# Gated linear attention and a token/channel mixer on one core: batch 0 by token slot, its u made transposed, another token order, other weight pieces, a new order of the work

## The chip, the cores and the metric

The kernel runs on one core of a Trainium2 chip. The core has TensorE (PE in the profile; its weight loads are PEld), VectorE (DVE), ScalarE (ACT), GpSimd (POOL) and SyncE (SP), each with its own in-order queue, and DMA engines that move data between HBM and SBUF. TensorE writes to PSUM, which the kernel splits into eight banks of 512 fp32 values per partition. The metric is the device time of one launch in microseconds (us); a kernel's time is the median of its runs.

## The reference

Four batches, eight heads, 768 tokens, head size 48. First a recurrence with a decay per key channel, then a mixer over tokens and channels, both with a residual:

```python
state = zeros((B, H, D, D))
for t in range(S):
    state = alpha[:, :, t, :, None] * state + einsum('bhd,bhe->bhde', k[:, :, t], v[:, :, t])
    y[:, :, t] = einsum('bhd,bhde->bhe', q[:, :, t], state)
x = y.transpose(0, 2, 1, 3).reshape(B, S, H * D)              # 4 x 768 x 384
h = relu(x.T @ w_tok1) @ w_tok2                               # 768 -> 256 -> 768, per batch
u = x + h.T
out = u + relu(u @ w_ch1) @ w_ch2                             # 384 -> 1536 -> 384
```

Inputs and output are fp32; the kernel computes its products in bf16 with fp32 sums.

## The kernel before

**Attention.** The tokens of a batch are cut into three chunks of 256 (`n` = 0 to 11 over four batches; batch 0 has chunks 0, 1 and 2). Partition p of a chunk holds tokens 2p and 2p+1, its two *slots*; partitions 0 to 63 are the first half of 128 tokens, 64 to 127 the second. Per chunk: load alpha, k, q, v (`ld_at`, `ld_kt`, `ld_qt`, `ld_vt`, 384 KB each); logarithms of alpha on ACT (`ln`); running sums of them by a triangular matmul (`cum`, in batch 0 `cumw` for both slots at once); exponentials `E` and `IE`; keys and queries scaled by them (`kk`, `qq`, line 700); transposes of both (`trk`, `trq` on PE in chunks 0 to 5; `dk`, `dq` by DMA later) and copies into `tpk` and `tpq` (`evk`, `evq`, later `pq`); scores `G` per half of 128 tokens, multiplied with a mask on DVE into `gtm` (`mask`, line 770); `y` = masked scores times v, plus the earlier state's part (`ia`, `ib`); `x` is the copy of y in bf16. `K` sums keys times values per half. The state is either `s` (times the decay, line 837), or an add (`sa`, line 841) followed by a product (`sm`, line 844) where there is an earlier state.

So that K and y can contract over all 128 partitions of one half of the tokens, values and keys of a half must lie on 128 partitions: `vs` (two copies of 64 partitions of v) and `ka`, `kb`, `kc` (of the scaled keys) move them, on ACT, POOL or DVE.

**Mixer.** Per batch: `t1` (12 matmuls, x with w_tok1) and `ht` (relu); `t2` (12, ht with w_tok2); `u` (add of x, on DVE); the transpose of u into `ut`; `c1` (24 groups of three matmuls of 384 columns, each a channel block `mc` of 12 and a half of the tokens) and `rt` (relu, on ACT or DVE, line 873 or 875); `c2` (six token blocks in four groups of three) and `o` (add of u, line 911); `st` (store). In batch 0 the transpose of u runs on PE (`up`, line 894) with three copies; in the others it is a DMA transpose (`ux`, line 729).

**Weights** are loaded as fp32 in 16 pieces of 384 KB into the buffers of the inputs and cast to bf16 (`ldw`, `cw`). w_ch1 comes in six pieces of 128 rows by 768 columns, so a channel block of c1 waits for three pieces.

**Order.** All instructions stand in one written list (`ORDER`), where each name ends in its engine: t is PE, s ACT, v DVE, g POOL, y SP. An engine takes its own names in this order and waits at each for its inputs; so a name that waits holds back all of its engine's names behind it. `BUFS` gives the buffer of every value in the order of first use: an instruction that writes into a buffer also waits for the last user of what was there (a PSUM bank, an input buffer). `shared` (line 732) makes POOL's SBUF work and the DVE's that is marked with `port` take turns in list order. All loads and DMA transposes, and some stores, are issued from SP's queue, the other stores from ACT's. `f1` to `f12` are dummy matmuls on zeros (the fill; up to four of 384 columns in fp32 and the rest of 512 in bf16), each before the matmul that it names; `fN` has N // 3 in fp32, each of which the profile records as two, and N % 3 in bf16.

## Time and profile before

| | |
|---|---|
| median of 3 runs | 163.48 us (163.34 to 164.39) |
| span of the profiled execution, first to last instruction | 160.5 us |
| the profiled execution's own time beside its span | not given; the median lies 3.0 us above the span |
| PE busy | 154.6 us, 96% |
| DVE, ACT, POOL busy | 114.9, 97.8, 80.8 us |
| HBM read, written | 25.17 MB, 4.72 MB |
| granted TensorE clock | 1.00 |

A row of the profile names the line, the engine, the operation, what it writes and reads (`out<-in`, buffer numbers left out) with partitions x elements and types, how many there were, then busy time, mean duration in ns, the idle time of the engine before them and what ended it. In rows in order of time the first two numbers are the start in the span and the length in us, and the bracket holds the idle time before. Matmuls are pipelined, and their recorded lengths overlap: their rate is read from their starts. Line 643 is a helper that issues most matmuls of the attention, so these are told apart by their tiles.

### The profile page before, as it was taken

Reading aid. Unit: us, or ns where it says so; the run is one execution under the profiler, and the core shown is the slowest. Engines: PE = TensorE matmul, PEld = TensorE weight load, DVE = VectorE, ACT = ScalarE, POOL = GpSimd, SP = SyncE. Lnnn points to the kernel's source line nnn. Section 1 sums busy time; section 2 is a strip of 40 time slices with the busy share of each in tenths; the row PEclk is TensorE's granted clock in tenths of the full one; section 3 lists DMA queues with packets and bytes.
Section 4 is the critical chain, followed back from the end, with each engine's and each line's share of the span. In section 5 each row is a group of like instructions: output and inputs, shape, how many; then the busy total and the mean of one; then the engine's idle time right before and its main releaser. Section 6 shows DMA issues by size and latency. Waiting matters only on the chain.

```text
span 160.5 us, 3971 instructions
## 1 busy us (share of the span) xinstructions
PE 154.6 (96%) x1563; PEld 97.1 (60%) x1563; DVE 114.9 (72%) x206; ACT 97.8 (61%) x179; POOL 80.8 (50%) x94
## 2 busy tenths in 40 slices
...
GB/s 122 320 324 317 317 374 311 339 333 306 316 347 324 275 278 272 210 228 319 241 202 298 239 315 204 217 196 134 196 21 62 87 79 169 49 49 53 49 129 116
DMA packets 76130, 35.05 MB, mean 218 GB/s; under 512 B 70352, under 2 KB 74320, under 8 KB 76112
## 3 DMA queue, kind: packets, MB, share of 16 engines
q1 hardware_dynamic: 73808, 31.76, 74.1%
...
q14 instruction: 6, 0.05, 0.1%
HBM read 25.17 MB, written 4.72 MB: 186 GB/s over the span
## 4 chain that ended last, share of the span: by engine, by line
PE 61%; DMA 12%; DVE 6%; ACT 6%; SPq 6%; POOL 4%; issue 3%; DVEq 0%; POOLq 0%
PE ps L907 22%; PE ps L902 21%; PE ps L643 11%; DMA in<-in_v_dram 6%; SPq L584 6%; DMA out_dram<-o 4%; PE ps L878 3%; PE ps L883 2%; DMA ut<-u 2%; DVE pkk L700 2%; DVE gtm L770 1%; PE ps L712 1%; DVE rt L875 1%; POOL vb L746 1%; POOL pkq L700 1%
## 5 line engine op out<-in xcount | busy, mean ns | idle before, releaser
L907 PE MATMUL ps<-wc,rt 128*128 128x384 bf16 (+1 forms) x300 | 52.4, 319 | 0.0
L902 PE MATMUL ps<-ut,wc 128*128 128x384 bf16 x288 | 50.3, 326 | 0.1
L902 PEld LDWEIGHTS <-wc 128*128 128x128 bf16 x288 | 27.1, 98 | 17.9 <-DMA ut<-u 0.6
L907 PEld LDWEIGHTS <-rt 128*128 128x128 bf16 x300 | 27.8, 98 | 16.0
L873 ACT ACTIVATE rt<-ps 128x384 bf16<-128x384 f32 x47 | 21.4, 492 | 23.6 <-PE ps L902 23.3
L875 DVE TENSOR_SCALAR rt<-ps 128x384 bf16<-128x384 f32 x49 | 25.6, 551 | 9.1 <-PE ps L902 8.9
L770 DVE TENSOR_TENSOR gtm<-ps,mk 128x1024 bf16<-128x1024 f32 x24 | 28.5, 1218 | 3.1 <-PE ps L643 2.8
L911 DVE TENSOR_TENSOR o<-ps,u 128x384 f32<-128x384 f32 (+1 forms) x25 | 13.2, 536 | 12.6 <-PE ps L907 10.1
L700 POOL TENSOR_TENSOR pkk<-in,IE 128x768 bf16<-128x768 f32 x8 | 14.5, 1817 | 3.3 <-DVE ss L844 2.3
L745 ACT CAST x<-ps 128x384 bf16<-128x384 f32 x20 | 9.2, 479 | 11.1 <-PE ps L643 9.5
L887 DVE TENSOR_TENSOR u<-ps,x 128x384 bf16<-128x384 f32 x24 | 12.0, 550 | 3.1 <-PE ps L883 2.5
L746 POOL CAST vb<-in 64x384 bf16<-64x384 f32 (+1 forms) x14 | 8.3, 594 | 10.4 <-DMA in<-in_v_dram 4.7
L692 POOL TENSOR_TENSOR in<-in,in 128x384 f32<-128x384 f32 x8 | 8.0, 1000 | 10.5 <-DVE u L887 3.8
L643 PE MATMUL ps<-rt 128*128 128x512 bf16 (+1 forms) x29 | 12.1, 515 | 1.1 <-DVE rt L541 1.1
L745 ACT CAST vb<-in 64x384 bf16<-64x384 f32 (+1 forms) x18 | 11.4, 634 | 0.8 <-DMA in<-in_v_dram 0.3
L700 POOL TENSOR_TENSOR pkq<-in,E 128x768 bf16<-128x768 f32 x6 | 10.9, 1818 | 0.6 <-DMA tpk<-pkq 0.3
L878 PE MATMUL ps<-x,wt 128*128 128x384 bf16 x48 | 11.0, 325 | 0.0
L844 POOL TENSOR_TENSOR ss<-tmp,E 128x384 bf16<-128x384 f32 x10 | 8.3, 833 | 4.2 <-DVE in L628 3.9
L841 DVE TENSOR_TENSOR tmp<-ps,ss 128x384 f32<-128x384 f32 x16 | 8.8, 552 | 1.8 <-PE ps L643 0.6
L883 PE MATMUL ps<-ht,wt 128*128 128x384 bf16 x48 | 9.1, 326 | 0.0
L643 PE MATMUL ps<-vb,gtm 128*128 128x48 bf16 x192 | 8.2, 183 | 0.2 <-DVE gtm L770 0.2
L643 PE MATMUL ps<-tpq,tpk 48*64 48x128 bf16 (+1 forms) x288 | 7.9, 218 | 0.4 <-POOL tpq L746 0.3
...
## 6 DMA issues: line engine op xcount, KB each, us to landing
...
```

What stands on the lines that cost most here:

```text
L643: return self.pe.matmul(out, lhsT=lhsT, rhs=rhs, start=start, stop=stop, skip_group_check=True)
L700: self.shared(self.eng[e].tensor_tensor(self.t(dst)[:, :, h0:h1, 0:D], self.t(src)[:, h0:h1].rearrange("p h s d -> p s h d"), bass.AP(tens ...
L745: return self.act.copy(d, s)
L770: self.nc.vector.tensor_tensor(self.t(gtm)[:, hf, :, :], self.pair(gp).rearrange("p a (j t) -> p (a j) t", t=128), bass.AP(tensor=m.tensor ...
L873: self.act.activation(d, s, AF.Relu)
L875: self.nc.vector.tensor_scalar_max(d, s, 0.0)
L878: self.pe.matmul(self.bank(bank)[:, 0:HD], lhsT=self.wt1[:, kc, m * 128 : m * 128 + 128], rhs=self.t(x), start=(kc == 0), stop=(kc == NS - 1))
L883: self.pe.matmul(self.bank(bank)[:, 0:HD], lhsT=self.wt2[:, kc, i * 128 : i * 128 + 128], rhs=self.t(hts[kc]), start=(kc == 0), stop=(kc = ...
L887: self.nc.vector.tensor_tensor(self.t(u)[:, i % 3], self.bank(bank)[:, 0:HD], self.t(x), ALU.add)
L902: self.pe.matmul(self.bank(bank)[:, 0:HD], lhsT=self.wc1[:, kc, mc * 128 : mc * 128 + 128], rhs=self.t(ut)[:, 3 * half : 3 * half + 3, kc, ...
L907: self.pe.matmul(self.bank(bank)[:, 0 : cz - ca], lhsT=self.t(rts[mc][0])[:, i * 128 : i * 128 + 128], rhs=self.wc2[:, mc, ca:cz], start=( ...
L911: self.nc.vector.tensor_tensor(self.t(o)[:, ca:cz], self.bank(bank)[:, 0 : cz - ca], self.t(u)[:, i % 3, ca:cz], ALU.add)
```

## The change

- **Chunks 0 to 2 by token slot** (`SLOT`). Scores, mask, K and y are made per slot rather than per half: K and y contract over 64 partitions each (one half's tokens of one slot); `vs`, `ka`, `kb` and `kc` go from these chunks. The matmul counts per chunk: G 32 on 64 x 64 tiles for 16, K 16 for 8 (8 for 4 in chunk 2), y 32 for 16. The earlier state is added to K in PSUM by a matmul with the identity (`A`, four in all), so each state is one product `s` on DVE.
- **u of batch 0 transposed** (`UDIR`). `tt` computes the transposed h directly (ht as weights, w_tok2 moving), onto the transposed x that `xa` puts into the bank by identity matmuls (18 of 128 columns); `ut` is a copy of that bank (six). u in natural order, which only `o` reads, comes from two DMA transposes (`un`) on SP. `up` and the adds `u` of batch 0 go.
- **Token order.** Within 128 tokens the even ones come first, then the odd ones, all through x, u and the output's rows: the copies `evq` and `pq` take the same pattern as `evk`; masks, the rows of w_tok1 (two loads of 64 partitions per piece), the columns of w_tok2 and the rows of each store follow.
- **Weight pieces.** w_tok2 is cut by token halves; w_ch1 into six pieces of 256 columns by all rows, so a channel block waits for one piece.
- **A new ORDER and BUFS** for the whole kernel. The attention of chunk 0 now starts alone, behind f12 and f4; many operations change engine.

The diff, cut to its core:

```diff
-UP = (0,)
+UP = ()
+UDIR = (0,)
...
-SLOT = ()
+SLOT = (0, 1, 2)
...
-                    emit=lambda e: g.trwev(e, tpk, bk, n not in SLOT))
+                    emit=lambda e: g.merged(e, tpk, g.bank(bk).bitcast(BF16)))
...
-            evq = O("evq", either(dve(1024 * 1.065), act(1024 * 1.34)), 9, writes=[tpq], reads=[bq], preds=[trq],
-                    emit=lambda e: g.qev(e, tpq, g.bank(bq).bitcast(BF16)))
+            evq = O("evq", either(dve(1024, True), act(1024)), 9, writes=[tpq], reads=[bq], preds=[trq],
+                    emit=lambda e: g.merged(e, tpq, g.bank(bq).bitcast(BF16)))
...
+        if b in UDIR:
+            ut, us, uts = V("ut"), [], []
+            for half in range(2):
+                evs = []
+                for j in range(NM):
+                    bank = V("one")
+                    tx = x[3 * half : 3 * half + 3]
+                    xa = P.op(f"xa_{b}_{half}_{j}", pe([128] * 3), m0 + (1700 + 900 * half + 60 * j) * sc, writes=[bank],
+                              reads=[v for v, _ in tx], preds=[o for _, o in tx],
+                              emit=lambda e, bank=bank, tx=tx, j=j: g.xadd(bank, [v for v, _ in tx], j))
+                    o = P.op(f"tt_{b}_{half}_{j}", pe([384] * 2), m0 + (1900 + 900 * half + 330 * j) * sc, writes=[bank],
+                             reads=[h for h, _ in hts], preds=[h for _, h in hts] + [xa, wl[("wt2", half)]],
+                             emit=lambda e, bank=bank, half=half, j=j: g.tok2t(bank, half, j, [h for h, _ in hts]))
+                    evs.append(P.op(f"ut_{b}_{half}_{j}", either(act(384), dve(384)), m0 + (1950 + 900 * half + 330 * j) * sc,
+                                    writes=[ut], reads=[bank], preds=[o],
+                                    emit=lambda e, bank=bank, half=half, j=j: g.utev3(e, ut, bank, half, j)))
+                uts.append(evs)
                 u = V("u")
-            bank = V("one")
-            o = P.op(f"t2_{b}_{i}", pe([384] * 2), m0 + (1900 + 330 * i) * sc, writes=[bank],
-                     reads=[h for h, _ in hts], preds=[h for _, h in hts] + [wl[("wt2", p)] for p in range(2)],
-                     emit=lambda e, i=i, bank=bank: g.tok2(bank, i, [h for h, _ in hts]))
-            uo = P.op(f"u_{b}_{i}", dve(384), m0 + (1950 + 330 * i) * sc, writes=[u], reads=[bank, x[i][0]], preds=[o],
-                      emit=lambda e, i=i, bank=bank, u=u: g.uadd(u, i, bank, x[i][0]))
-            us.append((u, uo))
-        ut = V("ut")
-        uts = []
-        if b in UP:
-            for p in range(3):
+                un = P.op(f"un_{b}_{half}", {"SP": (1240.0, 1240.0)}, m0 + 6000 * sc, writes=[u], reads=[ut], preds=evs,
+                          emit=lambda e, u=u, half=half: g.unat(u, ut, half), dma=("x", 1450.0, 1180.0, 480.0))
+                us += [(u, un)] * 3
...
-                         reads=[ut], preds=(uts[0:2 + half] if b in UP else [uts[half]]) + [wl[("wc1", p)] for p in ((0, 1, 2) if mc < 6 else (3, 4, 5))],
+                         reads=[ut], preds=(uts[half] if b in UDIR else uts[0:2 + half] if b in UP else [uts[half]]) + [wl[("wc1", mc // 2)]],
...
-                          reads=[bank, us[i][0]], preds=[prev],
+                          reads=[bank, us[i][0]], preds=[prev, us[i][1]],
...
-ld_at1y ld_at0y ln1s ln0s f8_cumw1t f1_cumw1t cumw1t IE1s cumw0t IE0s ld_vt0y E0s vb0g vs0_0g vs1_0v ld_kt0y kk0v
-f8_trk0t f1_trk0t trk0t E1s ld_qt0y qq0v ka0s kb0s kc0v f1_trq0t trq0t ld_kt1y kk1v K0t evq0s s0_0v ld_vt1y vb1s
-f1_trk1t trk1t ld_at2y evk0v ln2s f2_G0_0t G0_0t ld_qt1y ka1g sa1_0v f4_cumw2t cumw2t mask0_0v vs0_1s kb1g kc1g vs1_1s
-K1t sm1_0g qq1v sa0_1v sm0_1v G1_0t ld_kt2y IE2s E2s trq1t evq1s ib0t mask1_0v f3_y1_0t y1_0t y0_0t evk1v G0_1t sa1_1v
-ld_qt2y x1_0s mask0_1v G1_1t ld_vt2y x0_0s vb2s kk2g trk2t kc2s ldw_wt10y qq2g cw_wt10s f2_ia1t ia1t mask1_1v evk2s
-trq2t ld_at3y vs1_2g ldw_wt11y evq2v ib1t y1_1t y0_1t vs0_2g ldw_wt21y sm1_1g P3g K2t sa0_2v sm0_2g x0_1s t1_0_0_0t
-f1_G0_2t G0_2t ldw_wt20y G1_2t cw_wt20g t1_0_1_0t mask0_2v x1_1s t1_0_1_1t ld_at4y ld_kt3y t1_0_1_2t lnP3s cum3t
-cw_wt11s IE3s ia2t y0_2t x0_2s t1_0_0_1t t1_0_0_2t E3s t1_0_0_3t mask1_2v t1_0_1_3t ib2t y1_2t ldw_wc14y t1_0_1_4t
-x1_2s t1_0_0_4t f1_t1_0_1_5t t1_0_1_5t ht_0_1v P4g cw_wt21s t1_0_0_5t ht_0_0s f3_t2_0_0t t2_0_0t t2_0_1t u_0_0v ln13s
...
+ld_at0y ln0s f12_cumw0t f4_cumw0t cumw0t IE0s ld_vt0y vb0v ld_kt0y kk0v f6_K0t f1_K0t K0t E0s ld_at1y ln1s cumw1t E1s
+trk0t ld_qt0y qq0v s0_0v trq0t evk0s evq0v f3_G0_0t G0_0t ld_qt1y qq1g f1_trq1t trq1t mask0_0v ld_kt1y IE1s ld_at2y
+ln2s G1_0t A1_0t evq1s cumw2t kk1v ld_kt2y IE2s kk2g trk1t mask1_0v evk1v E2s ib0t y0t G0_1t G1_1t ld_vt1y vb1s s1_0v
+x0_0v mask1_1v K1t A0_1t s0_1v trk2t ib1t ia1t A1_1t mask0_1v s1_1v ld_qt2y x1_0s qq2g ld_vt2y trq2t evq2v vb2s K2t
+A0_2t s0_2v evk2s G1_2t mask1_2v y1t ld_at3y P3g G0_2t mask0_2v ldw_wt10ay ldw_wt10by cw_wt10g lnP3s ln13s x0_1s
+ld_at4y cum3t t1_0_1_0t x1_1s xa_0_0_0t t1_0_1_1t t1_0_1_2t ldw_wt11by ia2t t1_0_0_0t t1_0_0_1t t1_0_0_2t ib2t
+ldw_wt11ay y2t IE3s P4g cw_wt11g t1_0_0_3t lnP4s xa_0_0_2t E3s x0_2s t1_0_1_3t xa_0_0_1t t1_0_1_4t x1_2v t1_0_1_5t
+ht_0_1v t1_0_0_4t t1_0_0_5t ht_0_0s xa_0_1_2t xa_0_1_1t xa_0_1_0t ldw_wt21y cw_wt21g cum4t ln14s r13s tt_0_1_2t
+ut_0_1_2v tt_0_1_1t tt_0_1_0t ut_0_1_0v ldw_wt20y cw_wt20g tt_0_0_1t tt_0_0_0t ut_0_1_1s IE4s ut_0_0_1s E4s tt_0_0_2t
+ut_0_0_2v ldw_wc15y cw_wc15g c1_0_10_1t rt_0_10_1v ldw_wc10y cw_wc10g c1_0_1_1t rt_0_1_1v ld_kt3y ldw_wc14y k0a3g kk3v
+c1_0_0_1t rt_0_0_1v ut_0_0_0s c1_0_0_0t c1_0_1_0t ld_vt3y vb3v cw_wc14s c1_0_9_0t c1_0_9_1t c1_0_11_0t trk3t kb3v
+rt_0_9_1v c1_0_8_0t c1_0_8_1t rt_0_0_0s ka3s r14s rt_0_9_0v evk3v ldw_wc13y cw_wc13g vs0_3g c1_0_7_1t rt_0_7_1v
+rt_0_11_0s vs1_3s kc3s rt_0_1_0s ld_qt3y q0r3g qq3v c1_0_6_0t c1_0_6_1t rt_0_6_1v K3t s0_3v ldw_wc12y cw_wc12s
+c1_0_4_0t trq3t evq3v rt_0_8_1s rt_0_8_0s rt_0_4_0s sa1_3v ld_kt4y c1_0_5_1t rt_0_5_1s rt_0_6_0v ldw_wc11y cw_wc11s
+c1_0_4_1t c1_0_5_0t rt_0_5_0v G0_3t mask0_3v G1_3t c1_0_2_1t rt_0_2_1s k0a4g kk4g kb4s rt_0_4_1s mask1_3v c1_0_11_1t
+trk4t ld_at5y P5g lnP5s c1_0_3_0t ld_qt4y q0r4g qq4g rt_0_3_0v c1_0_3_1t rt_0_3_1v evk4v ldw_wc20y cw_wc20s ln15s
+c1_0_10_0t ib3t c1_0_2_0t rt_0_2_0s rt_0_10_0s ka4s y1_3t rt_0_11_1v x1_3v c1_0_7_0t trq4t cum5t E5s evq4v ldw_wc21y
+IE5s cw_wc21g c2_0_0_0t sm1_3g ldw_wc22y cw_wc22v rt_0_7_0v ldw_wc24y ldw_wc23y c2_0_5_0t G0_4t mask0_4v ld_qt5y G1_4t
+mask1_4v r15s cw_wc23s c2_0_3_0t ld_vt4y c2_0_3_1t ld_kt5y kc4g c2_0_0_1t c2_0_5_1t cw_wc24s c2_0_5_2t c2_0_0_2t ia4t
+y0_3t vb4s vs0_4s q0r5g qq5v c2_0_3_2t y0_4t vs1_4s K4t x0_3s ldw_wc25y cw_wc25s x0_4s trq5t un_0_1y evq5s k0a5v kk5v
+trk5t sa0_4v sm0_4g sa1_4v ld_vt5y c2_0_3_3t c2_0_5_3t o_0_5v c2_0_0_3t o_0_3v ld_kt7y c2_0_4_0t evk5s G0_5t mask0_5v
+G1_5t mask1_5v c2_0_2_0t c2_0_2_1t c2_0_2_2t ib4t vb5s vs0_5s sm1_4g vs1_5s y1_4t x1_4s kc5g K5t sa0_5v ld_vt6y
+ld_at6y st_0_3s c2_0_2_3t t1_1_1_0t t1_1_1_1t sm0_5v t1_1_1_2t t1_1_1_3t ia5t y0_5t x0_5v ib5t y1_5t x1_5s un_0_0y
+st_0_5s o_0_0v o_0_2v t1_1_0_0t ld_at7y t1_1_0_1t t1_1_0_2t t1_1_0_3t t1_1_0_4t t1_1_1_4t t1_1_1_5t t1_1_0_5t
...
-            w = self.w[0].rearrange("(c p) m -> p c m", p=128)
-            self.gated(dma(t.rearrange("p (c m) -> p c m", c=3), w[:, 3 * piece : 3 * piece + 3, :]), op)
+            w = self.w[0].rearrange("(c p s) m -> s p c m", p=64, s=2)[part]
...
+            w = self.w[1].rearrange("(c p) m -> p c m", p=128)
+            self.gated(dma(t.rearrange("p (c m) -> p c m", c=2), w[:, :, HD * piece : HD * piece + HD]), op)
...
-            c, h = piece % 3, piece // 3
-            self.gated(dma(t, self.w[2][128 * c : 128 * c + 128, 768 * h : 768 * h + 768]), op)
+            w = self.w[2].rearrange("(c p) m -> p c m", p=128)
+            self.gated(dma(t.rearrange("p (c m) -> p c m", c=3), w[:, :, 256 * piece : 256 * piece + 256]), op)
...
+    def rows(self, d):
+        return d.rearrange("(p s) c -> s p c", s=2)
+
     def store(self, e, o, b, i, ca, cz):
-        self.queue(e).dma_start(self.out[b, i * 128 : (i + 1) * 128, ca:cz], self.t(o)[:, ca:cz])
+        self.queue(e).dma_start(self.rows(self.out[b, i * 128 : (i + 1) * 128, ca:cz]), self.t(o)[:, ca:cz])
...
+    def merged(self, e, d, s):
+        self.copy(e, self.t(d).rearrange("p (g s t) -> p s g t", g=8, s=2), s.rearrange("p (s g t) -> p s g t", s=2, g=8))
...
+            r = slice(64 * h, 64 * h + 64)
+            dv.tensor_copy(self.mk[r, 0], c[r, r])
+            dv.tensor_copy(self.mk[r, 1], self.u2[r, r])
+            for d, t in ((0, self.us), (1, self.u2), (2, self.u2)):
+                dv.tensor_copy(self.mkw[r, d], t[r, r])
...
+                    at = j * 256 + hf * 128
                     self.mm(self.bank(gp, r)[hf * 64 : hf * 64 + 64, j * 128 : j * 128 + 128],
-                            tk[pr, (sl * 4 + j) * 128 + hf * 64 : (sl * 4 + j) * 128 + hf * 64 + 64],
-                            tq[pr, j * 256 + hf * 128 : j * 256 + hf * 128 + 128], True, True)
+                            tk[pr, at + sl * 64 : at + sl * 64 + 64], tq[pr, at : at + 128], True, True)
...
+    def xadd(self, bank, xs, j):
+        for i, x in enumerate(xs):
+            self.mm(self.bank(bank)[:, i * 128 : i * 128 + 128], self.t(x)[:, j * 128 : j * 128 + 128], self.idn, i == 0, False)
+
+    def tok2t(self, bank, half, j, hts):
+        for kc in range(NDT):
+            self.mm(self.bank(bank)[:, 0:HD], self.t(hts[kc])[:, j * 128 : j * 128 + 128],
+                    self.wt2[:, half, kc, :], False, kc == NDT - 1)
+
+    def utev3(self, e, ut, bank, half, j):
+        self.copy(e, self.t(ut)[:, 3 * half : 3 * half + 3, j, :], self.bank(bank)[:, 0:HD].rearrange("p (i t) -> p i t", i=3))
+
+    def unat(self, u, ut, half):
+        self.nc.sync.dma_start_transpose(self.t(u).rearrange("p i (j c) -> p (i j) c", j=NM),
+                                         self.t(ut)[:, 3 * half : 3 * half + 3].rearrange("p i j t -> p (i j t)"))
...
```

Functions that `SLOT` now calls and that the kernel before has unused:

```python
    def khalf(self, kps, pkk, vb, first):
        kk, vv = self.t(pkk), self.t(vb)
        for j in range(4):
            for sl in range(2):
                for hf, kp in enumerate(kps):
                    ph = slice(hf * 64, hf * 64 + 64)
                    self.mm(self.bank(kp)[:, 96 * j : 96 * j + 96], kk[ph, sl, 2 * j : 2 * j + 2, :],
                            vv[ph, sl, 2 * j : 2 * j + 2, :], j == 0 and sl == 0, (first and hf == 0) and sl == 1)

    def kadd(self, kp, s0):
        self.mm(self.bank(kp)[:, 0:HD], self.idn, self.t(s0), False, True)

    def yslot(self, yps, gtm, vb, first):
        gg, vv = self.t(gtm), self.t(vb)
        for h in range(H):
            for sl in range(2):
                for hf in range(2):
                    ph = slice(hf * 64, hf * 64 + 64)
                    self.mm(self.bank(yps[hf])[:, h * D : h * D + D], gg[ph, sl, 4 * (h % 2) + h // 2, :],
                            vv[ph, sl, h, :], first[hf] and h == 0 and sl == 0, h == H - 1 and sl == 1)
```

210 lines of the change are left out of this document (95 added, 115 removed), and 22 rows, old and new, of the table BUFS.

## The prediction

> **What bounds the kernel now.** I read the page's busy times first, then stretches of the span, then TensorE (PE) in order of time. The columns of the stretches are engine busy time with instruction counts, granted clock, DMA share and GB/s.
>
> ```profile
> PE 154.6 (96%) x1563; PEld 97.1 (60%) x1563; DVE 114.9 (72%) x206; ACT 97.8 (61%) x179; POOL 80.8 (50%) x94
> ```
>
> ```profile
> 5.00:10.00 5.00, 4.78 (x41) 2.36 (x40) 1.64 (x3) 4.30 (x7) 1.32 (x2) 1.00 1.16 321
> ...
> 20.00:25.00 5.00, 4.53 (x78) 3.18 (x77) 4.88 (x6) 4.74 (x10) 4.25 (x7) 1.00 1.10 365
> ...
> 30.00:40.00 10.00, 9.99 (x96) 6.66 (x95) 8.63 (x18) 9.12 (x16) 6.96 (x8) 1.00 1.06 326
> ```
>
> ```profile
> 27.73 2.28 PE L883 MATMUL ps<-ht,wt 128*128 128x384 bf16 x12
> 29.85 0.83 PE L894 MATMUL ps<-idn,u 128*128 128x128 bf16 x12
> ...
> 30.81 0.61 PE L712 MATMUL ps<-idn,pkk 128*128 128x128 bf16 x8
> 31.25 0.50 PE L894 MATMUL ps<-idn,u 128*128 128x128 bf16 x6
> 31.76 4.55 PE L902 MATMUL ps<-ut,wc 128*128 128x384 bf16 x27
> 36.14 0.61 PE L712 MATMUL ps<-idn,pkq 128*128 128x128 bf16 x8
> ...
> 39.05 0.33 PE L643 MATMUL ps<-vb,pkk 128*128 128x96 bf16 x4
> 39.21 0.33 PE L643 MATMUL ps<-vb,kt 128*128 128x96 bf16 x4
> 39.38 0.65 PE L902 MATMUL ps<-ut,wc 128*128 128x384 bf16 x3
> 39.97 0.62 PE L643 MATMUL ps<-tpq,tpk 48*128 48x128 bf16 x16
> 40.52 4.56 PE L902 MATMUL ps<-ut,wc 128*128 128x384 bf16 x27
> 44.92 0.61 PE L712 MATMUL ps<-idn,pkq 128*128 128x128 bf16 x8
> ```
>
> Starts give the true rate: 27 matmuls of 384 columns in 31.76 to 36.14 are 0.162 us each, and each row starts where the one before stops issuing. From 27.73 on PE is full. Before that, "busy" includes dummy matmuls (the fill, `ps<-rt`) and waiting. So there are two parts: a **start** up to the first channel matmul (c1, L902) at 31.76, which chains of small steps set, and a **full stretch** to 157, whose length is PE work. All c1 of batch 0 is issued by 44.92. In the start VectorE (DVE) has 4.88 of 5 us at 20 to 25, so DVE is its bound there.
>
> **The change, part by part.** These rows price the steps (groups by line; then the first microseconds in order).
>
> ```profile
> L770 DVE TENSOR_TENSOR gtm<-ps,mk 128x1024 bf16<-128x1024 f32 x24 | 28.5, 1218 | 3.1 <-PE ps L643 2.8
> ...
> L700 POOL TENSOR_TENSOR pkq<-in,E 128x768 bf16<-128x768 f32 x6 | 10.9, 1818 | 0.6 <-DMA tpk<-pkq 0.3
> ...
> L700 DVE TENSOR_TENSOR pkk<-in,IE 128x768 bf16<-128x768 f32 x4 | 3.8, 955 | 0.6 <-POOL in L692 0.5
> ...
> L745 ACT COPY tpk<-ps 128x1024 bf16<-128x1024 bf16 x3 | 3.0, 1010 | 0.0
> ...
> L746 POOL CAST wc<-in 128x768 bf16<-128x768 f32 x3 | 2.6, 859 | 1.4 <-DVE pkk L700 1.1 <-DMA in<-in_moe_w_ch_dram 0.4
> ...
> L683 ACT ACTIVATE E<-ps 128x800 f32<-128x800 f32 x3 | 2.4, 836 | 0.0
> ...
> L837 DVE TENSOR_TENSOR ss<-ps,E 128x384 bf16<-128x384 f32 x4 | 2.2, 552 | 0.9 <-PE ps L643 0.9
> ...
> L746 DVE COPY tpk<-ps 128x1024 bf16<-128x1024 bf16 x3 | 2.0, 679 | 0.0
> ...
> L746 DVE COPY tpq<-ps 128x1024 bf16<-128x1024 bf16 x1 | 1.3, 1305 | 0.0
> ```
>
> ```profile
> 1.06 4.21 PE L643 MATMUL ps<-rt 128*64 128x384 f32 x7 [1.06 <-DVE rt L541]
> ...
> 7.34 2.26 PE L643 MATMUL ps<-rt 128*64 128x384 f32 x7
> ```
>
> ```profile
> 4.28 0.84 ACT L637 ACTIVATE la<-in 128x768 bf16<-128x768 f32 x1 [2.19 <-DMA in<-in_alpha_dram]
> ...
> 5.47 0.84 ACT L637 ACTIVATE la<-in 128x768 bf16<-128x768 f32 x1 [0.35 <-DMA in<-in_alpha_dram]
> ...
> 6.32 0.81 ACT L687 ACTIVATE IE<-ps 128x768 f32<-128x768 f32 x1
> ...
> 6.91 1.39 POOL L746 CAST vb<-in 128x768 bf16<-128x768 f32 x2 [4.11 <-DMA in<-in_v_dram]
> ...
> 23.17 2.36 DVE L770 TENSOR_TENSOR gtm<-ps,mk 128x1024 bf16<-128x1024 f32 x2
> ```
>
> *Loads.* The first three inputs are in at about 4.25, 5.45 and 6.9; after that 384 KB at 321 GB/s is 1.2 us each. The new order starts with chunk 0: at0, vt0, kt0, at1, qt0, so qt0 is there at about 9.4.
>
> *First chunk.* The fill ahead of cumw0 is f8 and f1 now (seven recorded matmuls: 4.21 us at the start, 2.26 later) and becomes f12 and f4, eleven. Seven run to 5.3, four more at 0.32 to 6.6. The first Ln ends at 5.12, so cumw0 starts 1.45 late. IE0 starts 1.2 after that Ln's end now (6.32), of which 0.05 is the way to PE; so 1.15 after cumw0: 7.75. On ACT, IE0, E0 and ln1 follow at some 0.8 each, to 10.1; cumw1 ends 11.2, E1 12.0, the copy evk0 (1.01) 13.0, so the first mask starts at 13.5. On DVE kk0 is 8.6 to 9.55, qq0 to 10.5, s0 to 11.05, evq0 12.1 to 12.8: 1.75 us idle between kk0 and that mask.
>
> *DVE from kk0 to the last mask of chunk 2.* 3 scalings at 0.955, 3 copies at 0.679 (evq0 loses the strided pattern that cost 1.305), 5 state products and one x at 0.552, 6 masks at 1.18 (2.36 for two): 2.9 + 2.0 + 3.3 + 7.1 = 15.3. From 8.6 with 1.75 idle: 25.65. Today's last mask ends at 25.53 (23.17 + 2.36). So this end stays where it is, although half-swap copies, k turns and add-then-multiply states leave chunks 0 to 2: they were on ACT, POOL and DVE, but masks and scalings stay, and the late first chunk takes what was saved.
>
> *From that mask to c1.* Now 25.53 to 31.76, 6.2 us: last y, x, t1, ht, t2, u, transposes `up`, ut. New: y2 to 26.3, x to 26.9, the last t1 to 27.55, ht to 28.25, while PE does xadd (18 of 128 columns, the same 0.056 as the 18 removed transposes) and cum4; twelve tt from 28.35 to 30.3, whose first half is copied out by 30.05. c1 starts at 30.2, 1.5 earlier: u and ut become one step. The first c1 needs only weight piece wc15, the 19th load instead of three up to the 22nd: about 26.8, cast (0.859) by 28.1, so weights don't set it. Four state adds of 0.162 and K2 (0.17 more) lie ahead of this point, in PE's idle time; if that cover went, 0.8.
>
> *PE work moved behind c1.* trk3 (0.44, 30.81 to 31.25) isn't done yet: **+0.45**. K and y become twice as many matmuls on 64 rows. Bounds: 0 if pairs overlap, or the work of K (0.33, 39.05 to 39.38) and of y once more, all but the last y in PE's idle time. The nearest row says overlap: 16 matmuls of G on 48 rows take 0.55 (39.97 to 40.52), while 8 transposes of that width take 0.44. I take 0. But those 0.55 also hold some 0.1 beyond 16 halves of 0.056. [...]
>
> *The c1 stage.* The stretch from 31.8 to 45 now:
>
> ```profile
> 31.80:45.00 13.20, 13.20 (x106) 8.22 (x107) 11.36 (x20) 11.71 (x22) 9.95 (x11) 1.00 1.03 323
> ```
>
> DVE 11.4 and ACT 11.7 of 13.2. The new order gives DVE kk3 and qq3 (+1.9) and evq3 (+0.7) and four relus fewer (-2.0): 12.0. ACT loses evq3 (-1.3), gains a cast (+0.86), a half-swap (+0.5) and four relus (+1.8): 13.5. A c1 bank is freed by its relu, so PE waits where one is queued late. Following the queues I find c1_0_0_0 behind ut_0_0_0 on ACT (0.1), c1_0_5_0 behind evq3 (0.2), c1_0_3_0 behind mask0_3 (0.3). **+0.6**; bounds 0 and 3.1 (ACT so dense that a wait hits every third group).
>
> *Queues.* On SP, ld_qt0 now waits for vb0 (it reuses vt0's buffer, free at 6.05) and ld_at2 for ln1 (10.1); every later load is queued behind them. Two loads are in flight each time, so I take 0; bound 0.6 each. wt1 in halves adds two issues. The two transposes `un` and the merged copies have these rows:
>
> ```profile
> ut<-u SPq DMA_TRANSPOSE x6, 3.0
> ```
>
> ```profile
> 68.03 1.33 SPq L729 DMA_TRANSPOSE ut<-u  x1
> ```
>
> ```profile
> 116.29 0.64 PE L643 MATMUL ps<-tpq,tpk 48*64 48x128 bf16 x32 [0.28 <-POOL tpq L746]
> ...
> 117.85 0.31 PE L643 MATMUL ps<-vb,gtm 128*128 128x48 bf16 x6
> ```
>
> Each `un` holds SP 1.3 and lands 3 later. Loads ahead of them are issued by about 47, and o_0_5, the first reader, comes about 54; behind it on DVE would stand o_0_3 and the masks of chunk 5. Cost 0, up to 1 if the loads run late. G on 64 x 64 tiles (0.64 for 32) costs what 16 of the other cost (0.62). POOL's copy of q is not shown in its new pattern: between DVE's 0.68 and today's 1.34; I keep 1.34. Row-permuted stores keep rows of 1.5 KB: 0. Later PE stops like the 0.28 here I take as equal, with -0.8 to +1.5 around it, since the whole order is new.
>
> *End.* Now the last add is half an output:
>
> ```profile
> 157.44 0.36 DVE L911 TENSOR_TENSOR o<-ps,u 128x192 f32<-128x192 f32 x1 [0.43 <-PE ps L907]
> ```
>
> In the new order o_3_5 (0.55) ends 0.1 after that add could start: **+0.1**.
>
> **Sum.** -1.5 + 0.45 + 0.6 + 0.1 = about -0.4 (rounded from -0.35). The span of 160.5 becomes 160.1; the median of the timed runs, 163.48, lies 3.0 above the span, which I leave unchanged: **163.1 us**, with 162.0 to 164.4 as its own range.
>
> **Rivals.**
> - *Short start, clean c1 stage (161.0).* If DVE's idle 1.75 vanishes (cumw0 not held by the fill) and no c1 waits: -3.0 + 0.45 + 0.1 = -2.5. For it: fewer ACT and POOL steps feed DVE. Against: the 4.21 us of seven fill matmuls.
> - *ACT bounds the c1 stage, slower (165.6).* ACT holds 13.5 us of work in about 13.9, in one fixed queue with weight casts that wait for loads. If PE stands 3.1 in place of 0.6: -1.5 + 0.45 + 3.1 + 0.1 = +2.1. It decides once the waits in 30 to 46 pass 2.6 us (+1.6). For it: 9.12 of 10 busy on ACT already; against: PE lost only tenths there with that.
> - *The change doesn't shorten the start (164.6).* If SP's new waits delay the loads by 1.2 to 2, c1 starts at 31.7 as now: +0.45 + 0.6 + 0.1 = +1.15.
> [...]
>
> **How the numbers follow.** Forecast 0.41, short start 0.24, ACT-bound 0.24, no shorter start 0.07, drains 0.04. One per cent, 1.6 us, is about what a measurement of this kernel can tell from no change. Below 161.85 lie the short start and a little of the forecast: 0.26; above 165.1 the ACT-bound case and edges of the others: 0.28; between, 0.46. The range 160.9 to 166.0 reaches to both outer cases and leaves some 0.2 outside.
>
> **What would show it.** cumw0 at 6.6 and the first mask near 13.5; the last mask of chunk 2 at 25 to 26; the first c1 at 30.2, with one copy step between tt and c1; trk3 behind it; waits of PE of 0.3 to 1 in 30 to 46, on relus of ACT; full PE after that; the last PE row 0.5 earlier than 157. Wrong would be: a start that ends with a load or cast as releaser, PE waiting over 2 us before 46, or stops over 1 us at a G whose `pq` comes late.

## Result and the profile after

The changed kernel takes **226.75 us** (median of 4 runs, 223.89 to 230.19) against 163.41 us for the kernel before on the same chip (162.3 to 164.39). The ratio is 1.381, with a 95% interval of 1.369 to 1.393. The profiled execution took 227.15 us, of which the span is 225.3 us. The forecast was 163.1 us, range 160.9 to 166.0. Executions of one kernel come in a faster and a slower kind (the 230.19 is a slower one, the other three lie within 223.89 to 227.15), and every ratio here compares the faster ones alone.

The page of the changed kernel: engines, granted clock by slices, and the head of the chain of waits.

```profile
PE 166.9 (74%) x1673; PEld 102.3 (45%) x1673; DVE 114.2 (51%) x208; ACT 89.9 (40%) x169; POOL 75.8 (34%) x82
...
PEclk9999699999996788999788996699999889999555
...
DMA 51%; PE 24%; POOL 7%; SPq 4%; DVE 3%; issue 3%; ACT 3%; ACTq 0%; DVEq 0%; POOLq 0%
```

PE was busy 96% and is busy 74%. In the chain, DMA's share is 51%, where it was 12%. Other than in the kernel before, the granted clock isn't full throughout: it is 0.80 to 0.95 over the stretches in which PE stands. Stretches of the span (busy time and count of PE, PEld, DVE, ACT, POOL, then clock, DMA share, GB/s) show where the time goes:

```profile
0.00:33.00 33.00, 28.68 (x420) 17.80 (x421) 20.28 (x50) 19.07 (x31) 13.55 (x19) 0.95 0.99 267
33.00:48.00 15.00, 15.00 (x139) 9.47 (x137) 14.02 (x25) 12.23 (x25) 10.55 (x11) 1.00 1.07 339
48.00:75.00 27.00, 19.56 (x210) 12.38 (x208) 16.62 (x26) 15.01 (x28) 8.47 (x11) 0.89 0.94 222
75.00:110.00 35.00, 25.27 (x235) 15.21 (x234) 17.30 (x30) 15.38 (x31) 17.80 (x16) 0.94 0.99 151
110.00:145.00 35.00, 23.04 (x215) 13.58 (x215) 15.26 (x24) 10.85 (x22) 16.50 (x17) 0.80 1.10 167
```

The channel stage of batch 0 (33 to 48) is full. The loss begins where the first outputs are stored. From the waits of the changed kernel (us in total, times, longest):

```profile
DVE o L943 <- DMA out_dram<-o: 46.5, 11, 6.6
...
PEld L934 <- DMA ut<-u: 9.2, 4, 3.6
```

The same wait in the kernel before:

```profile
DVE o L911 <- DMA out_dram<-o: 2.5, 3, 1.6
```

and a row of its list of DMA issues (count, KB each, median us from issue to landing):

```profile
out_dram<-o ACTq DMA_DIRECT2D x15, 192.0 KB, 1.8
```

The final addition waits 46.5 us in place of 2.5 for its three output buffers, that is, for stores to leave them. Everything behind it on DVE waits too. The chain of the changed kernel in order of time (start, length, what) shows stretches of 8.8 and 13.2 us that wait for stores, and after the first of them 8.0 us for a transpose of u:

```profile
61.84 8.84 DMA out_dram<-o
...
74.62 7.97 DMA ut<-u
...
96.55 13.16 DMA out_dram<-o
```

The DMA packets in the two traces say why. A store has 128 packets of 1536 B. In the kernel before some 13 of them are in flight, and a store that meets little other traffic is through in 0.64 us (median of all 0.66). In the changed kernel 2 are in flight, and it takes 4.0 to 7.2 us (median 5.0), though the median packet takes its 65 ns as ever: 64 packets one behind another, one every 0.062 us, make 4.0, while the other 64 go beside them. The 256 B packets of the transposes have a 95th percentile of 86 ns in place of 18. The traces name no engine, so it isn't shown that they meet the stores on the same ones.

The start, PE of the changed kernel in order of time:

```profile
6.20 0.65 PE L667 MATMUL ps<-la,u 128*128 128x384 bf16 x3
...
9.14 0.51 PE L667 MATMUL ps<-vb,pkk 64*128 64x96 bf16 x16
9.61 0.65 PE L667 MATMUL ps<-la,u 128*128 128x384 bf16 x3
...
25.37 0.50 PE L894 MATMUL ps<-x,wt 128*128 128x384 bf16 x1 [1.25 <-POOL wt L763]
...
30.94 2.11 PE L667 MATMUL ps<-wt,ht 128*128 128x384 bf16 x12
32.89 3.41 PE L934 MATMUL ps<-ut,wc 128*128 128x384 bf16 x19
```

and DVE and POOL:

```profile
22.92 2.35 DVE L786 TENSOR_TENSOR gtm<-ps,mkw 128x1024 bf16<-128x1024 f32 x2
```

```profile
24.49 0.82 POOL L763 CAST wt<-in 128x768 bf16<-128x768 f32 x1 [1.41 <-DMA in<-in_moe_w_tok_dram]
```

The first sum comes at 6.20 (forecast 6.6), the last mask of chunk 2 ends at 25.27 (25.65), but the first channel matmul comes at 32.89 (30.2; the expectations below call it 33.05), and w_tok1 lands late: PE waits 1.25 us for its cast at 25.37, and the cast 1.41 us for the load. So two things had to be explained: some 50 us from the stores (e1 and e5 below), and the rest.

### The profile page after: what moved, and what is told of

Read it like the earlier page. It is cut to its first block, busy times and chain, and to the rows that moved or that the text cites. A ratio compares the mean times of both kernels' runs of the same rounds, so it can differ in the third digit from the quotient of the medians.

```text
span 225.3 us, 4182 instructions
## 1 busy us (share of the span) xinstructions
PE 166.9 (74%) x1673; PEld 102.3 (45%) x1673; DVE 114.2 (51%) x208; ACT 89.9 (40%) x169; POOL 75.8 (34%) x82
## 4 chain that ended last, share of the span: by engine, by line
DMA 51%; PE 24%; POOL 7%; SPq 4%; DVE 3%; issue 3%; ACT 3%; ACTq 0%; DVEq 0%; POOLq 0%
DMA out_dram<-o 27%; DMA ut<-u 11%; PE ps L934 10%; PE ps L667 8%; DMA tpk<-pkq 4%; DMA in<-in_v_dram 4%; DMA in<-in_moe_w_ch_dram 3%; DMA in<-in_moe_w_tok_dram 2%; PE ps L939 2%; SPq L604 2%; POOL pkq L724 2%; SPq L742 2%; PE ps L894 2%; PE ps L899 2%; POOL pkk L724 2%
## 5 line engine op out<-in xcount | busy, mean ns | idle before, releaser
L939 PE MATMUL ps<-wc,rt 128*128 128x384 bf16 (+1 forms) x300 | 55.9, 330 | 9.3 <-DVE o L943 4.6
L934 PE MATMUL ps<-ut,wc 128*128 128x384 bf16 x288 | 55.9, 347 | 8.1 <-DMA ut<-u 4.9
L943 DVE TENSOR_TENSOR o<-ps,u 128x384 f32<-128x384 f32 (+1 forms) x25 | 13.1, 538 | 54.8 <-DMA out_dram<-o 46.5
L786 DVE TENSOR_TENSOR gtm<-ps,mk 128x1024 bf16<-128x1024 f32 x18 | 21.1, 1216 | 2.0 <-PE ps L667 2.0
L724 POOL TENSOR_TENSOR pkq<-in,E 128x768 bf16<-128x768 f32 x8 | 14.5, 1816 | 13.0 <-ACT E L707 9.8
L652 POOL TENSOR_TENSOR in<-in 128x384 f32<-128x384 f32 x9 | 8.9, 995 | 19.5 <-DVE in L716 7.6
L720 POOL TENSOR_TENSOR in<-in,lf 128x384 f32<-128x384 f32 x9 | 9.0, 997 | 15.2 <-DMA in<-in_q_dram 12.8
L724 POOL TENSOR_TENSOR pkk<-in,IE 128x768 bf16<-128x768 f32 x6 | 10.9, 1815 | 3.4 <-ACT IE L711 3.2
L667 PEld LDWEIGHTS <-tpk 48*64 48x64 bf16 (+1 forms) x336 | 6.6, 115 | 11.7 <-DMA tpk<-pkk 8.2
L667 PE MATMUL ps<-rt 128*64 128x384 f32 (+1 forms) x19 | 8.5, 574 | 1.0 <-DVE rt L566 1.0
L899 PEld LDWEIGHTS <-wt 128*128 128x128 bf16 x36 | 3.7, 108 | 10.9 <-DVE o L943 5.5
```

The source lines that it names most:

```text
L667: return self.pe.matmul(out, lhsT=lhsT, rhs=rhs, start=start, stop=stop, skip_group_check=True)
L724: self.shared(self.eng[e].tensor_tensor(self.t(dst)[:, :, h0:h1, 0:D], self.t(src)[:, h0:h1].rearrange("p h s d -> p s h d"), bass.AP(tens ...
L786: self.nc.vector.tensor_tensor(d, self.pair(gp).rearrange("p a (j t) -> p (a j) t", t=128), bass.AP(tensor=m.tensor, offset=m.offset, ap=[ ...
L899: self.pe.matmul(self.bank(bank)[:, 0:HD], lhsT=self.wt2[:, i // 3, kc, i % 3 * 128 : i % 3 * 128 + 128], rhs=self.t(hts[kc]), start=(kc = ...
L934: self.pe.matmul(self.bank(bank)[:, 0:HD], lhsT=self.wc1[:, kc, mc * 128 : mc * 128 + 128], rhs=self.t(ut)[:, 3 * half : 3 * half + 3, kc, ...
L939: self.pe.matmul(self.bank(bank)[:, 0 : cz - ca], lhsT=self.t(rts[mc][0])[:, i * 128 : i * 128 + 128], rhs=self.wc2[:, mc, ca:cz], start=( ...
```

## The experiments

Unless a text says otherwise, "before" is the kernel before on the same chip, at 161.99 to 163.12 us. A kernel with whole stores writes its rows in another order; its work is the same.

### The stores

**e1_split.** The changed kernel, each store as two DMAs of 64 partitions:

```diff
-        self.queue(e).dma_start(self.rows(self.out[b, i * 128 : (i + 1) * 128, ca:cz]), self.t(o)[:, ca:cz])
+        d = self.rows(self.out[b, i * 128 : (i + 1) * 128, ca:cz])
+        for s in range(2):
+            self.queue(e).dma_start(d[s], self.t(o)[64 * s : 64 * s + 64, ca:cz])
```

> The changed kernel, with each store issued as two transfers of 64 partitions (even tokens, then odd ones) in place of one whose outer dimension is 2. Theory A (the stores: an outer dimension of 2 leaves 2 of 16 DMA engines to each 192 KB store, 64 packets of 0.062 us each = 4.0 us in place of 0.6, and loads and transposes queue behind them): nearly all of the 63 us go, 160 to 167 us, no wait of DVE for an output buffer over 2 us. Theory B (the new order and its colder TensorE clock cause it): over 200 us.

177.89 us (175.66 to 179.42), ratio 1.094 [1.087, 1.102]. One edit of the stores takes back 0.287 of the ratio, about 47 us, so the new order isn't the main cause. But it stays above the 160 to 167 expected. The wait falls:

```profile
DVE o L945 <- DMA out_dram<-o: 7.6, 4, 3.1
```

**e2, e3, e4.** The kernel before with nothing changed but the stores' outermost dimension, 2, 4 and 16:

```diff
-        self.queue(e).dma_start(self.out[b, i * 128 : (i + 1) * 128, ca:cz], self.t(o)[:, ca:cz])
+        d = self.out[b, i * 128 : (i + 1) * 128, ca:cz].rearrange("(p s) c -> s p c", s=2)
+        self.queue(e).dma_start(d, self.t(o)[:, ca:cz])
```

> The kernel before, with nothing but its stores changed to the outer dimension of 2 (its rows land in another order than the reference's). Theory A: as slow as the changed kernel or somewhat less, 195 to 235 us, with DVE waiting for output buffers for tens of us. Theory B: 163 to 165 us.

> As before_outer2, but an outer dimension of 4 (rows permuted in fours). Theory A, the outer dimension sets the number of DMA engines: packets of one store take about 2.0 us, four at a time; the kernel 163 to 180 us. If rows out of order were the cost, as slow as with 2: 195 to 235 us.

> As before_outer2, but an outer dimension of 16. Theory A: 16 engines again, 0.6 us per store, 163 to 165 us. If rows out of order were the cost: 195 to 235 us.

| outermost dimension | time, us | ratio to before | one store, us | packets in flight |
|---|---|---|---|---|
| 128 (before) | 162.38 | 1 | 0.6, 0.7 | 13 |
| 16 | 164.33 | 1.011 [1.006, 1.016] | 0.7, 0.9 | 12 |
| 4 | 192.39 | 1.183 [1.172, 1.193] | 2.0, 2.8 | 3.8 |
| 2 | 229.08 | 1.408 [1.399, 1.417] | 4.0, 5.0 | 2.0 |

The last two columns are from the packets of each trace, over its 23 whole stores: the shortest and the median time, and the median of the packets in flight. The wait of the addition, in e2, in e3 and in e4:

```profile
DVE o L912 <- DMA out_dram<-o: 45.9, 13, 7.8
```

```profile
DVE o L912 <- DMA out_dram<-o: 19.7, 9, 4.6
```

```profile
DVE o L912 <- DMA out_dram<-o: 4.9, 3, 2.1
```

So the kernel before becomes as slow as the changed kernel by this alone. Rows out of order aren't the cost, since 16 costs 1%. With 2 and 4, as many packets are in flight as the outermost dimension is long; with 16 and 128 some 12 to 13. That the dimension sets how many engines carry a store, as the expectations have it, is the author's reading of these counts: no trace names a packet's engine, and no number between 4 and 16 was run. The time for 4 was dearer than expected (163 to 180); that the transposes wait behind the stores is a likely reason, but was not tried.

### The rest: which part of the new order costs 10 us?

**e5_after_plain_store.** The changed kernel with the store line of the kernel before.

> The changed kernel with each store as the kernel before has it: one DMA of 128 rows in partition order (the rows of the output land in even-odd order; nothing else differs). It asks where the 15 us come from by which the changed kernel with its stores halved (177.89 us) stood above the kernel before. Theory A, the two DMAs for each store are to blame (25 more issues of 0.5 to 0.6 us on ACT and SP, each 64 partitions wide): 163 to 167 us here. Rival B, the rest of the change is to blame (later first channel matmul, loads and transposes that come late in the new order): 172 to 178 us, with the stalls of TensorE at 64 to 74 and 85 to 105 us still there.

172.8 us (171.75 to 175.74), ratio 1.063 [1.051, 1.075]. Halving the stores costs 5 us, and **10 us belong to the rest of the change**: both answers are part of it. The 5 us need not be the double issue alone, for the packets of the halved stores take 107 ns (median) in e1 in place of 65. Stretches of the kernel before, then of this one:

```profile
0.00:33.00 33.00, 30.69 (x325) 17.39 (x326) 23.93 (x54) 27.58 (x43) 19.40 (x31) 1.00 1.02 305
...
62.00:75.00 13.00, 13.00 (x120) 8.00 (x119) 11.53 (x23) 9.92 (x21) 10.08 (x9) 1.00 0.99 244
...
90.00:110.00 20.00, 19.93 (x192) 12.41 (x190) 14.95 (x27) 11.51 (x26) 13.10 (x13) 1.00 1.00 225
```

```profile
0.00:33.00 33.00, 28.16 (x423) 17.28 (x424) 20.50 (x51) 19.29 (x32) 13.88 (x20) 1.00 1.03 274
...
62.00:75.00 13.00, 11.28 (x67) 6.31 (x66) 8.47 (x17) 6.52 (x15) 5.89 (x7) 0.87 1.12 274
...
90.00:110.00 20.00, 17.81 (x205) 11.66 (x204) 13.44 (x22) 10.72 (x23) 11.32 (x12) 0.91 1.00 246
```

PE stands in three places, and in two of them the clock falls as well. Of the 9.6 us by which the span of e5 exceeds that of the kernel before, 2.7 are longer PE work (157.3 us busy for 154.6, at a mean clock of 0.98) and 6.9 are standing. By 33 us the DMA has moved 274 GB/s in place of 305, with its engines as busy: 9.08 MB against 10.07.

**e6 and e7: w_tok1 whole.** The two loads of 64 partitions become one of 128 (e6 puts the second at the later half's place, e7 at the earlier):

```diff
-            w = self.w[0].rearrange("(c p s) m -> s p c m", p=64, s=2)[part]
+            w = self.w[0].rearrange("(c p) m -> p c m", p=128)
```

> The kernel of the run e5_after_plain_store with each of the two w_tok1 pieces loaded by one DMA of 128 partitions in place of two of 64 (the weight rows then stand in natural order, so the result is another; the work is the same). Theory S, the split loads make w_tok1 late and the late w_tok1 sets the start of the channel stage (33.05 us in the changed kernel against 30.2 forecast): the first channel matmul comes 1 to 2 us earlier than in e5_after_plain_store, and the time falls by as much. Rival R, the loads behind ld_at3 come late because ld_at3 waits for its buffer, whatever the pieces: the first channel matmul moves by less than 0.5 us.

172.96 us (170.85 to 174.4), ratio 1.060 [1.050, 1.070]: no gain in time, with the first channel matmul at 32.1 (32.5 in e5). But here SP stood from 18.65 to 23.19 us ahead of the second piece, so e7 repeats it.

> The kernel of e5_after_plain_store (172.8 us) with each w_tok1 piece loaded by one DMA of 128 partitions at the place of the first of its two halves (e6_plain_wt1_whole had put the second piece at the place of the later half and handed its buffer numbers to other tiles, so that SP stood from 18.65 to 23.19 us). In e5 the DMA packets of 384, 1024 and 1536 B took 36 to 38, 79 and 126 ns between 21 and 26 us, against 22, 46 and 65 ns elsewhere, and by 33 us 9.08 MB had moved against 10.07 MB in the kernel before. Theory D, the 64-partition loads make the packets slow, and what is behind at 33 us is missing later because the DMA engines are busy up to 110 us: packets back at 22, 46 and 65 ns, at least 9.5 MB by 33 us, first channel matmul at 31.5 or earlier, time 168 to 171 us. Rival R, the dip has another cause: under 9.3 MB by 33 us, time 172 to 174 us.

170.62 us (one run at 167.21, three at 170.58 to 171.02; no ratio), so the time isn't settled by this run. The start came about as expected. Packets of 384, 1024 and 1536 B are back at medians of 22, 46 and 65 ns from 20 us on, as they are in e6, 9.56 MB are moved by 33 us, and the channel stage begins at 30.8. In e5 the means between 21 and 26 us are 30, 76 and 108 ns; the expectation's 36 to 38, 79 and 126 are those of single microseconds in it. So packets beside the loads of 64 partitions are slow, and they aren't beside whole loads. Counted from the first sum of the same trace, the channel stage begins 24.8 to 27.2 us later in the seven traces with w_tok1 in halves and 23.7 to 25.1 in the eight with whole pieces in place, 1.7 us earlier in the mean. Why packets are slow beside loads of 64 partitions, no run here shows.

**e8_plain_stores_early.** On ACT, the stores of the first two outputs ahead of casts:

```diff
-... vb5s vs0_5s sm1_4g vs1_5s y1_4t x1_4s ... st_0_3s ... x1_5s un_0_0y st_0_5s o_0_0v
+... st_0_5s st_0_3s vb5s vs0_5s sm1_4g vs1_5s y1_4t x1_4s ... x1_5s un_0_0y o_0_0v
```

> The kernel of e5_after_plain_store (172.8 us) with the stores of the first two output tiles (issued on ACT at 59.76 and 61.84 us, 2.5 and 5 us behind the additions that made them, because casts stand ahead of them on ACT) moved ahead of three casts on ACT, so that they are issued at about 57.3 us. If the wait of the addition o_0_0 for its buffer (2.3 us on DVE, ending at 64.37) is what holds t2 of batch 1 and lets TensorE stand 1.7 us at 64 to 66 us: the wait goes, the channel stage of batch 1 starts 1.5 to 2.5 us earlier (72.6 to about 70.6), and the time falls by 1 to 3 us. Rival, the loads are the bound there: the stage starts earlier, but the transposes at 85 to 97 us end as late as now, and the time stays within 0.7 us.

169.69 us (169.39 to 171.3), ratio 1.046 [1.040, 1.051]: about 3 us, as expected, and the stage of batch 1 begins at 71.35 in place of 72.59. DVE of e5, then of e8:

```profile
64.37 1.02 DVE L943 TENSOR_TENSOR o<-ps,u 128x384 f32<-128x384 f32 x2 [2.32 <-DMA out_dram<-o]
```

```profile
62.45 1.02 DVE L955 TENSOR_TENSOR o<-ps,u 128x384 f32<-128x384 f32 x2 [0.63 <-DMA u<-ut]
```

In these two traces the gain is in the clock: PE is busy 154.8 us in place of 157.3, at a mean clock of 1.00 in place of 0.98, and stands no less (13.3 us of the span, 12.8 in e5).

**e9_plain_no_un.** Without the two DMAs `un`:

```diff
-                un = P.op(f"un_{b}_{half}", {"SP": (1240.0, 1240.0)}, ...
-                us += [(u, un)] * 3
+                us += [(ut, evs[-1])] * 3
```

> The kernel of e5_after_plain_store (172.8 us) without the two transposing DMAs un that bring u of batch 0 back into rows; the final additions of batch 0 read the transposed u as it is (a tile of the same shape, so the same work on other numbers). Each un moves 0.29 MB in 1152 packets of 256 B, at 26 ns each 1.9 us of all 16 engines, and SP holds 2.0 and 2.5 us on the issues. Forecast in the prediction: they cost nothing (0). Theory D, the DMA engines are busy up to 110 us and everything that a load feeds moves back by what they carry more: time 168 to 170 us. Rival, they are covered: 171.8 to 173.8 us.

172.37 us (one run at 168.27, three at 172.11 to 173.15; no ratio). This decides nothing; e18 comes back to it.

### Do the gains add up?

**e10, e11, e12: three edits at once.** e7 and e8, and `ux_1_0y` moved up to right behind `u_1_0v`; e11 also with the fill f8 and f1; e12 with halved stores and w_tok1 in halves.

> The kernel of e5_after_plain_store (172.8 us) with three edits at once: w_tok1 whole (e7: 170.6), the two stores early on ACT (e8: 169.7), and the transposing DMA ux of batch 1's first half issued before three loads instead of behind them (in e8 TensorE stands 2.22 us for it at 69.1 to 71.4, and SP took 2.92 us to issue it at 66.09 behind five loads; in the kernel before it took 1.29 us at 64.68 with no load ahead of it since 60.9). Theory, the excess of the new order is a row of waits behind loads, each worth about what it shows and adding up: 2.2 and 3.1 and 1.5 to 2, so 165.5 to 167.5 us, channel stage of batch 1 starting at 68 to 69. Rival, what one wait gives is taken by the next (the transposes at 85 to 97 us): 168.5 to 170.5.

> The kernel of e10_plain_three_edits with the fill before the first cumulative sum of 8 and 1 rows as in the kernel before, in place of 12 and 4 (first cumulative sum at 5.17 us there, 6.20 in the changed kernel). Theory, the fill holds TensorE while the first load has landed: first cumulative sum 0.7 to 1.0 us earlier and the time 0.5 to 1.0 below e10. Rival, the sum waits for its logarithms anyway: less than 0.3 us either way.

> The whole computation with rows in their places: the kernel of e1_split (each store as two DMAs of 64 partitions, 177.9 us) with the early stores, the early ux and the short fill; w_tok1 stays in halves, since its rows must stand as they do. If the gains add up as in e10: 177.9 less 3.1, less 1.5 to 2, less 0.5 to 1, so 171.5 to 173 us, still above the kernel before (162.4). Rival, the double issues on ACT eat the early stores: 174.5 to 177.

174.61 us (ratio 1.067 [1.059, 1.075]), 176.43 (1.089 [1.082, 1.097]) and 180.28 (1.108 [1.103, 1.113]): all worse than the kernels that they build on (e8, and e1 for e12), and all three expectations missed. SP, DVE and PE of e10:

```profile
66.00 1.24 SPq L757 DMA_TRANSPOSE ut<-u  x1
67.35 0.53 SPq L615 DMA_DIRECT2D in<-in_k_dram  x1
```

```profile
72.51 0.96 DVE L735 TENSOR_TENSOR pkk<-in,IE 128x768 bf16<-128x768 f32 x1 [6.08 <-POOL in L727]
...
74.18 1.02 DVE L914 TENSOR_TENSOR u<-ps,x 128x384 bf16<-128x384 f32 x2
```

```profile
75.25 9.70 PE L945 MATMUL ps<-ut,wc 128*128 128x384 bf16 x42 [5.98 <-DVE u L914]
```

SP issued nothing between 60.0 and 66.0, since the moved transpose waited for u. The load of k 6 behind it was issued at 67.35 (at 59.77 in e14, where the transpose stands in its old place), DVE stood 6.08 us for it, and the last two additions of u stood behind that.

Behind the stop the clock is lower too. These 42 matmuls take 9.70 us, with a granted clock of 0.50 from 75 to 80 us; in e18, after a stop of 1.79, they take 7.00 at a clock of 1.00 (its row stands in the next part). Stops of 3.4 us and more ahead of this stage (the changed kernel, e7, e10, e11, e12) are all followed by a clock of 0.50 to 0.61 for some 4 us or more, and the 42 matmuls take 8.7 to 9.7. Shorter ones differ: 2.28 us in e13 brought 0.50, and 2.27 us in e14 didn't.

The fill did what was expected of it at the start: the channel stage of batch 0 begins at 29.2 in e11 and at 30.6 in e10. Yet e11 is slower than e10, clear of the intervals: PE stands 7.0 us for u in place of 6.0.

**e13, e14, e15: without the moved transpose.**

> The kernel of e5_after_plain_store (172.8 us) with w_tok1 whole (e7: 170.6) and the two stores early on ACT (e8: 169.7), the transposing DMA where the new order has it. If the gains add up: 172.8 less 2.2 less 3.1, so 166.7 to 168.3 us. If the loads set the pace from 60 to 100 us whatever starts earlier: 169 to 170.5.

> The kernel of e13_plain_two_edits with the fill of 8 and 1 rows before the first cumulative sum. In e11 the channel stage of batch 0 began 1.4 us before that of e10 (29.2 against 30.6) by this edit alone. If the start counts: 1 to 1.6 us below e13. If it is taken back by the waits for loads at 60 to 100 us: within 0.5 of e13 or above it.

> The whole computation with rows in their places: halved stores (e1: 177.9 us) with the two stores early on ACT and the short fill, the transposing DMA where the new order has it. By e8 and e14: 177.9 less 3.1 less 1.4, so 172.5 to 174.5 us. If the doubled issues on ACT and SP set the pace instead: 176 to 178.

169.69 us (ratio 1.042 [1.035, 1.049]), 169.75 (1.042 [1.035, 1.049]) and 176.25 (1.086 [1.078, 1.093]). e13 and e14 are no better than e8, so the gains don't add up: a start of the channel stage at 29.2 us (e14) in place of 31.8 (e8) is worth nothing at the end. e15, with rows in their places, gains 1.6 us on e1 in place of 3.4 to 5.4; with w_tok1 still in halves its channel stage begins at 32.2. SP and PE of e14 show where PE stands, and the last row is the transpose of the same place in the kernel before:

```profile
66.20 2.89 SPq L758 DMA_TRANSPOSE ut<-u  x1
```

```profile
71.42 7.17 PE L946 MATMUL ps<-ut,wc 128*128 128x384 bf16 x42 [2.27 <-DMA ut<-u]
...
95.77 0.64 PE L679 MATMUL ps<-tpq,tpk 48*64 48x128 bf16 x32 [2.57 <-DMA tpk<-pkk]
```

```profile
64.68 1.29 SPq L729 DMA_TRANSPOSE ut<-u  x1
```

**e16, e17: loads behind the transposes.** e16 moves the loads of alpha 8 and 9 and of q 6; e17 also those of alpha 10 and 11, behind the transpose of k 8.

```diff
-... ld_at9y ka6s ld_at8y ld_qt6y vs0_6v t2_1_3t u_1_3v ux_1_0y ...
+... ka6s vs0_6v t2_1_3t u_1_3v ux_1_0y ld_at9y ld_at8y ld_qt6y ...
```

> The kernel of e14_two_edits_short_fill (169.75 us) with the loads of alpha 8 and 9 and q 6 issued right behind the transposing DMA of u of batch 1's first half in place of ahead of it (k 6 stays ahead, other than in e10). If the transpose behind loads is what holds the channel stage of batch 1: it lands 3 to 4 us after its issue in place of 5.17, the stage starts at 69 to 70 in place of 71.42, and the time falls by 1 to 2 us. If the loads set the pace: the later loads take it back, the time stays within 0.7 or rises.

> The kernel of e16_loads_behind_ux with the loads of alpha 10 and 11, and what works on them on POOL and ACT, moved behind the transposing DMA of k of chunk 8 (issued at 88.62 us, 7.11 us to its landing, TensorE standing 2.57 us for it). If transposes behind loads hold the rest: the wait is gone or under 0.8 us and the time is 1.5 to 2.5 us below e16. If the loads set the pace: within 0.7 us of e16 or above it.

174.07 us (ratio 1.062 [1.051, 1.074]) and 175.22 (1.073 [1.065, 1.081]). The transpose of e16 is issued in 1.29 us and the stage starts at 70.0, as the first theory wants. But q 6 is issued at 69.22 in place of 64.97, and PE stands for a relu that is queued on DVE behind the scaling of q 6:

```profile
76.38 0.96 DVE L735 TENSOR_TENSOR pkq<-in,E 128x768 bf16<-128x768 f32 x1 [5.95 <-POOL in L663]
```

```profile
77.86 5.82 PE L945 MATMUL ps<-ut,wc 128*128 128x384 bf16 x27 [5.24 <-DVE rt L902]
```

In e17 the wait for the transpose of k 8 is down to 0.94 us (2.57 in e14), and PE stands 2.7 us for a state at 105 us instead. So **each move of u's transpose ahead of loads lost more on one of these loads than it gained**: on k 6 in e10, on q 6 in e16. An order that moves the loads of alpha 8 and 9 alone was not tried. That loads set the pace from 60 to 100 us fits these runs and the DMA share (1.13 to 1.16 there in e14, 0.97 to 1.06 before), but no run changes the loads' own speed there.

**e18_mended_no_un.** e14 without `un`.

> The kernel of e14_two_edits_short_fill (169.75 us) without the two transposing DMAs un of batch 0's u; the final additions of batch 0 read the transposed u as it is, as in e9 (other numbers, the same work). If the loads set the pace and un is what puts them behind: 20.8 MB or more without un's share by 70 us, the wait for the transposing DMA of u at 71 us shorter, time 166 to 168 us. If un is covered as forecast (0): 169 to 170.5.

167.15 us (166.18 to 167.19), ratio 1.029 [1.024, 1.033], against 1.042 for e14: `un` costs some 2 us. The bytes came out lower than expected: without any transposes 19.9 MB by 70 us, where e14 has 19.6 and the kernel before 20.0. So what else is moved comes somewhat earlier, though this trace's channel stage of batch 0 begins later (30.4; 29.2 in e14).

## Why the prediction was wrong

**The step that failed is "Row-permuted stores keep rows of 1.5 KB: 0."** The rows do stay 1.5 KB, and a packet still takes 65 ns. What changed is the pattern's outermost dimension, 128 to 2, which stands in the diff (`"(p s) c -> s p c", s=2`), and with it the packets of a store that are in flight (2 in place of 13). Its price is 5.0 us per store (median) in place of 0.66, and as three output buffers gate the additions, (1.381 - 1.063) x 163 = 52 us of the 63. The term had no bounds and no rival, so the range missed too. Had I asked what a store costs with two packets in flight, the row of before (192 KB, 1.8 us to its landing) and 128 packets of 0.065 us would have given 64 x 0.065 = 4.2 us per store; that a dimension of 2 leaves two in flight, only the runs show. e2 shows it by itself in the kernel before (5.0 us per store, ratio 1.408).

**The second is "Later PE stops like the 0.28 here I take as equal, with -0.8 to +1.5 around it".** With the store mended this is +10 us (e5). The parts that runs name:

- two early stores stood behind casts on ACT: 3 us (e8), as the clock falls less (a mean of 1.00 in place of 0.98);
- the transposes `un`, forecast 0 to 1: open in e9, some 2 us in e18;
- the late start, which the sum had at 30.2 and the trace has at 32.89. "wt1 in halves adds two issues" and "weights don't set it" failed at w_tok1: its halves cost 1.7 us in the mean of 15 traces. From the first sum to c1 the forecast was 30.2 - 6.6 = 23.6 us; with whole pieces it is 23.7 to 25.1, so the rest of that working was nearly right. But the 3.6 us that e14 took back (32.89 to 29.25) are worth nothing at the end.

The clock is a cost that the sum had no term for: it was 1.00 throughout before, and the 42 matmuls behind a stop of 5.98 us took 9.70 us (e10), 2.7 more than the 7.00 behind one of 1.79 (e18).

What stays, 1.029 or 4.6 us in e18, is PE standing, 4.0 us of it behind two transposing DMAs:

```profile
69.95 7.00 PE L942 MATMUL ps<-ut,wc 128*128 128x384 bf16 x42 [1.79 <-DMA ut<-u]
...
93.94 0.64 PE L675 MATMUL ps<-tpq,tpk 48*64 48x128 bf16 x32 [2.20 <-DMA tpk<-pkk]
```

What makes these two late was not found, so the cause of this part stays open.

**A premise fell with it:** that the full stretch to 157 is one "whose length is PE work". PE stands there for transposes and loads, and e14 shows that an earlier start is no gain. The DMA share of 1.03 to 1.16 stood in the quoted rows, and the working made no use of it. The 3.0 us that it added to the span was off too: the changed kernel's profiled execution lies 1.85 above its span.

**What held.** The fill at the start holds the first sum (6.20; 6.6 forecast, and 6.15 to 7.48 in the nine traces with that fill), and a shorter one brings the channel stage 1.4 us forward (e11); the last mask ends at 25.27; the merged u and ut follow with one copy step; `trk3` runs behind c1. The c1 stage stayed full (15.00 of 15 us): +0.6 was too much, and the rival "ACT bounds the c1 stage" is out (in e18, with an earlier start, PE is busy 14.21 of 15 us there). What stands behind the 0.04 of "drains" no run shows. What the traces show is the length of the new blocks: sixteen K matmuls on 64 rows start at 9.14 and the next group at 9.61, 0.47 us, against 0.33 for eight of 128 rows, and the eight of chunk 2 take 0.45 against 0.16 for four. That is 0.1 to 0.3 per block, where the sum took 0; its cause isn't shown. But the last mask didn't come later for it, so little of it lay on the path. "The change doesn't shorten the start" was given 0.07 and its start came true, with loads that come late. For 1.7 us of that the cause was another, though: the halved loads of w_tok1 and their slow packets, where it had named SP's new waits.
